# Four nested products instead of two in the last two groups of a token-mixing product, with operand sums on GpSimd

## The chip, the cores and the metric

The kernel runs on one core of one Trainium2 chip. The metric is the time of one execution in device microseconds. Each timed run gives one number, and the median of the runs stands for the kernel. The profile is one further execution, taken by the hardware profiler.

## What is computed

The reference is a linear attention block followed by a gated mixer, on 2048 tokens of width 512. Cut to the part that the change touches (`A` is the attention, `ln` a layer norm):

```
h  = x + A(ln(x))                                  # 2048 x 512
z  = gelu(ln(h) @ w_in)                            # 2048 x 1792
z1 = z[..., :Fh];  z2 = ln(z[..., Fh:])            # Fh = 896 columns each
g  = einsum('ts,sf->tf', w_sp, z2) + b_sp[:, None] # 2048 x 2048 times 2048 x 896
h2 = h + (z1 * g) @ w_out                          # 896 x 512
```

The product with `w_sp` mixes tokens. It is the largest product of the kernel, and it is the one that the change works on.

## The kernel before

All data stay in SBUF between the stages. Tokens are cut into 16 tiles of 128. The stages follow each other and overlap at their seams: attention (about the first 65 us), the product with `w_in` (to about 130 us), then the mixing product and the product with `w_out`, interleaved, to the end.

**The mixing product.** The 16 output tiles of `g` are taken as eight pairs (i, i+8), and two pairs make a group. `MIX` names the order: the groups are tiles (0, 1), (2, 3), (7, 4), (5, 6), each with its partner 8 higher. `mix` (L1042) computes one group. For each pair it uses a Strassen-Winograd scheme on 2 x 2 blocks: seven block products instead of eight. A block product of one pair is 8 matmuls of 128 x 448 columns, accumulated in a PSUM bank. The blocks of the left matrix are `wt[i]` and `wt[i+8]` (transposed `w_sp`) and their sums `sa`; those of the right matrix are `z2` and its sums `zt1`, `zt2`, `zt4`. The sums of operands are made by VectorE (DVE) with `comb` (L861), which adds or subtracts two bf16 tiles in SBUF. ScalarE (ACT) copies PSUM banks where a partial result is needed twice.

**Nesting.** A block product that both pairs of a group do against the same right block can be nested once more: `nested` (L1017) treats the two tiles as one 2 x 2 problem, and does 7 quarter products of 4 matmuls of 128 x 224 columns. It needs four sums of the left operands (`u`, tiles named nu, 512 elements per partition each), four sums of the right operand (`v`, tiles named nv, 896 elements each, made once by `quarter_sums`, L1010), four PSUM copies by ACT, and two additions in PSUM by DVE (L1026). `NEST` (L969) is a bit mask for each group: bit 1 nests the product of the first blocks, bit 2 nests the product of the sums `sa` with `zt1`. Before, it is (0, 3, 3, 3): none in the first group, two products in each later one.

**Gates.** A finished quarter of `g` gets its bias and is multiplied into `z1`. `gate` (L995) does that in one DVE instruction from PSUM (L997). `gate_p` (L1002) adds a bias-carrying copy `p` that ACT made (L1070), in one DVE instruction from PSUM (L1005), and multiplies in a second one in SBUF (L1006). A finished row of `z1` is transposed to `zgT` by a DMA on SyncE's queue (SP).

**Output product.** `mo_pair` (L1110) multiplies two `zgT` tiles with `w_out`, again by a seven-product scheme, in banks 6 and 7; its DVE evacuations are L1127 and L1139. Its operand sums (tiles us) are made by `comb` too. The last pair goes through `mo` (L1101).

**What sets the order.** Every operation is recorded first, with the operations that it depends on (data, and reuse of the same SBUF or PSUM place). `ORDER` (L16) is a packed list, written out in advance, of the sequence in which all recorded operations are emitted; each engine runs its own operations in that order. Waits come from the recorded dependencies. So a change of the operations needs a new list, and the new list may move anything. GpSimd (POOL) does small statistics of the layer norms up to about 120 us and nothing after.

The quarter sums lie in places that are dead by then: `nv1` in that of `win1`, `nv5` in that of `hnT`.

Of the kernel before, what the change touches and what calls it, by code (L numbers as in the profile page):

```python
# [252 lines left out]
def bass_sequential_preLN__linear_attn_block__mixer_gmlp__prompt_kernel(  # L253
# [14 lines left out]
    H = 32  # L268
# [733 lines left out]
    def gate_p(n, c, b, p):  # L1002
# [14 lines left out]
    def nested(X, Y, xa, xb, z, u, v, p):  # L1017
        X0, X1, Y0, Y1 = (bank(q, HQ, f) for q in (X, Y) for f in (0, HQ))
        r11, r12, r21, r22 = (x_[:, k:k + H4, :] for x_ in (xa, xb) for k in (0, H4))
        comb(u[0], r21, r22, ALU.add)  # L1020
        comb(u[1], u[0], r11, ALU.subtract)
        comb(u[2], r11, r21, ALU.subtract)
        comb(u[3], r12, u[1], ALU.subtract)
# [12 lines left out]
        copy(Y0, Y1)  # L1036
        add(Y1)
        prod(X1, u[3], z[:, H4:HT, HQ:HW], **onto)
        add(X1)
        prod(Y0, r22, v[3], **onto)  # L1040

    def mix(ia, ib, nest):  # L1042
        ss = range(HT)
        sets = ((ia, 0), (ib, 1))
        Y = {}
        for i, c in sets:
            Y[i] = tuple(wt[n][:, s:s + HT, :] for n in (i, i + HT) for s in (0, HT))
# [39 lines left out]
    DH2 = D // 2  # L1087
# [70 lines left out]
    wout_sums()  # L1158
# [36 lines left out]
```

## Time and profile before

| | |
|---|---|
| median of 3 runs | 227.19 us (227.16 to 227.52) |
| profiled execution | 227.34 us |
| its span, first to last instruction | 225.6 us |
| TensorE (PE) busy | 217.9 us, 97% |
| DVE busy | 193.5 us, 86% |
| ACT busy | 130.8 us, 58% |
| POOL busy | 51.3 us, 23% |
| granted TensorE clock | 1.00 in every stage |

A row of the timeline reads: start in us, length in us, engine, line, operation, output and inputs, shape, and how many equal instructions were merged. Matmuls are pipelined, so the length of a matmul row contains the end of the pipeline; what a group of matmuls costs is the distance from its start to the next start. The same holds for DVE rows, which overlap by some 0.08 us. A table by stage gives the busy time of each engine in stretches of the span. In the list of groups, "x16 | 10.9, 681" means sixteen instructions, 10.9 us busy in all, 681 ns each.

### The profile page before, as it was taken

Reading aid. Unit: us, or ns where it says so; the run is one execution under the profiler, and the core shown is the slowest. Engines: PE = TensorE matmul, PEld = TensorE weight load, DVE = VectorE, ACT = ScalarE, POOL = GpSimd, SP = SyncE. Lnnn points to the kernel's source line nnn. Section 1 sums busy time; section 2 is a strip of 40 time slices with the busy share of each in tenths; the row PEclk is TensorE's granted clock in tenths of the full one; section 3 lists DMA queues with packets and bytes.
Section 4 is the critical chain, followed back from the end, with each engine's and each line's share of the span. In section 5 each row is a group of like instructions: output and inputs, shape, how many; then the busy total and the mean of one; then the engine's idle time right before and its main releaser. Section 6 shows DMA issues by size and latency. Waiting matters only on the chain.

```text
span 225.6 us, 3738 instructions
## 1 busy us (share of the span) xinstructions
PE 217.9 (97%) x1311; PEld 123.0 (54%) x1325; DVE 193.5 (86%) x441; ACT 130.8 (58%) x256; POOL 51.3 (23%) x134
## 2 busy tenths in 40 slices
PE   8999999999989999999999999999999999999995
PEld 7534444453334444545555555766667667665653
DVE  3898855699989999999999999998899867497784
ACT  5686745479979999999773436624126222414111
POOL 2454400000368475786720000000000000000000
DMA  5836479937453255588930446999086109220663
GB/s 164 251 93 147 81 213 256 218 73 167 114 119 70 57 102 78 119 180 159 187 128 0 87 97 122 164 189 163 6 147 105 46 0 120 51 42 32 169 145 99
DMA packets 73906, 26.85 MB, mean 119 GB/s; under 512 B 63648, under 2 KB 73888, under 8 KB 73888
## 3 DMA queue, kind: packets, MB, share of 16 engines
q1 hardware_dynamic: 73184, 26.03, 54.9%
q10 hardware_dynamic: 704, 0.59, 0.8%
q8 instruction: 10, 0.16, 0.3%
q14 instruction: 8, 0.07, 0.1%
HBM read 6.95 MB, written 2.10 MB: 40 GB/s over the span
## 4 chain that ended last, share of the span: by engine, by line
PE 83%; DMA 6%; DVE 5%; ACT 3%; SPq 1%; issue 1%; ACTq 0%
PE psum L425 75%; PE psum L682 6%; DMA x<-in_A_x_dram 3%; DMA r<-rcp 2%; DMA zgT<-z1t 1%; DVE st L533 1%; DVE h L1139 1%; ACT ct L444 1%; ACT e L444 1%; SPq L790 1%; DVE z1t L997 1%; DVE pqT L815 1%; DVE psum L864 1%; SPq L455 1%; ACT z1t L444 0%
## 5 line engine op out<-in xcount | busy, mean ns | idle before, releaser
L444 ACT ACTIVATE psum<-psum 128x448 f32<-128x448 f32 (+2 forms) x67 | 28.5, 436 | 48.0 <-PE psum L425 40.8
L425 PE MATMUL psum<-z,wt 128*128 128x448 bf16 (+1 forms) x232 | 46.2, 343 | 0.0
L425 PEld LDWEIGHTS psum<-z,wt 128*128 128x128 bf16 x232 | 22.7, 98 | 17.3
L425 PE MATMUL psum<-win,hnT 128*128 128x448 bf16 x112 | 26.3, 353 | 0.0
L444 ACT ACTIVATE e<-psum 128x1024 bf16<-128x1024 f32 (+1 forms) x18 | 16.7, 929 | 14.1 <-PE psum L425 13.5
L444 ACT ACTIVATE z1t<-psum 128x448 bf16<-128x448 f32 (+1 forms) x24 | 16.2, 679 | 12.1 <-PE psum L425 10.1
L425 PE MATMUL psum<-zt,sa 128*128 128x448 bf16 (+1 forms) x116 | 21.7, 323 | 0.1
L425 PE MATMUL psum<-ws,hs 128*128 128x448 bf16 x72 | 18.9, 353 | 0.0
L425 PEld LDWEIGHTS psum<-win,hnT 128*128 128x128 bf16 x112 | 10.8, 98 | 10.6 <-ACT z L444 0.7
L425 PE MATMUL psum<-m,pqT 128*128 128x512 bf16 x63 | 14.7, 380 | 1.2 <-DVE pqT L815 1.0
L864 DVE TENSOR_TENSOR psum<-psum,p5z 128x448 f32<-128x448 f32 x24 | 15.0, 626 | 0.7 <-ACT z1t L444 0.5
L425 PE MATMUL psum<-wqkv,xnT 128*128 128x512 bf16 x62 | 14.9, 379 | 0.5 <-DMA wqkv<-in_A_wqkv_dram 0.5
L425 PE MATMUL psum<-xnT,wqkv 128*128 128x512 bf16 x61 | 15.0, 379 | 0.2
L682 PE MATMUL psum<-pk,xn 128*128 128x512 bf16 x63 | 15.1, 379 | 0.1
L444 ACT ACTIVATE z<-psum 128x896 bf16<-128x896 f32 x16 | 15.1, 955 | 0.1
L425 PEld LDWEIGHTS psum<-zt,sa 128*128 128x128 bf16 x116 | 11.3, 98 | 7.0
L997 DVE SCALAR_TENSOR_TENSOR z1t<-psum,b,z1t 128x448 bf16<-128x448 f32 x16 | 10.9, 681 | 3.7 <-PE psum L425 3.6
L557 POOL TENSOR_SCALAR st<-st 128x1 f32<-128x1 f32 x10 | 4.1, 410 | 42.7 <-ACT sh L444 37.1
L604 DVE TENSOR_SCALAR e<-e 128x1024 bf16<-128x1024 bf16 (+1 forms) x18 | 7.1, 395 | 7.7 <-ACT e L444 7.6
L425 PE MATMUL psum<-zt,wt 128*128 128x448 bf16 x64 | 13.4, 352 | 0.0
L533 DVE BATCH_NORM_STATS2 st<-x 128x6 f32<-128x512 bf16 x15 | 9.7, 680 | 4.1 <-DMA x<-in_A_x_dram 4.1
L425 PE MATMUL psum<-wout,zgT 128*128 128x256 bf16 (+1 forms) x71 | 13.0, 295 | 0.2 <-DVE h L1139 0.2
(145 smaller groups left out, 433.8 us busy)
## 6 DMA issues: line engine op xcount, KB each, us to landing
r<-rcp SPq DMA_DIRECT2D x16, 128.0 KB, 2.7
out_dram<-h SPq DMA_DIRECT2D x15, 128.0 KB, 1.8
win<-in_B_w_in_dram SPq DMA_DIRECT2D x2, 896.0 KB, 6.4
x<-in_A_x_dram SPq DMA_DIRECT2D x6, 256.0 KB, 4.0
wqkv<-in_A_wqkv_dram SPq DMA_DIRECT2D x2, 512.0 KB, 4.2
wout<-in_B_w_out_dram SPq DMA_DIRECT2D x1, 896.0 KB, 6.4
wo<-in_A_wo_dram SPq DMA_DIRECT2D x1, 512.0 KB, 4.9
wt<-in_B_w_sp_dram SPq DMA_TRANSPOSE x32, 3.9
```

The lines of the kernel that those rows point to most:

```text
L425: inst = pe.matmul(out_ap, lhsT=a, rhs=b, start=start and i == 0, stop=stop and i == len(pairs) - 1, **kw)
L444: return g.add("ACT", lambda ac: ac.activation(out_ap, in_ap, func, **kw), [in_ap, *extra], [out_ap] + ([accum] if accum is not None else []),
L455: return g.add(eng, lambda q: q.dma_start(out_ap, in_ap), [in_ap], [out_ap], cost=issue, lat=lat, dma=name, **k)
L533: dve(lambda v: v.bn_stats(s[:, 0:6], src[:, n, :]), [src[:, n, :]], [s[:, 0:6]], D)
L557: pool(lambda p: p.tensor_scalar(s[:, 2:3], s[:, 0:1], s[:, 0:1], -1.0 / (n * n), op0=ALU.mult, op1=ALU.mult), [s[:, 0:1]], [s[:, 2:3]], 240)
L604: dve(lambda v: v.tensor_scalar(e, e, 1.0, EPS_PHI, op0=ALU.min, op1=ALU.add), [e], [e], w * GW, acc=4)
L682: inst = pe.matmul(bank(CB[c]), lhsT=xn[:, i, c * P:(c + 1) * P], rhs=pk[:, i, :], start=i == 0, stop=i == NT - 1)
L790: g.add("SP", lambda q: q.dma_start(dst, src_ap), [rcp[:, i:i + w, :]], [dst], cost=700, lat=2200, dma=f"r{tg}{c // 2}").soft.add(win_last.i)
L815: dve(lambda v, q=q, r=r: v.tensor_tensor(q, q, r, ALU.mult), [q, r], [q], 2 * GW, acc=2)
L864: dve(lambda v: v.tensor_tensor(half(b), half(src), p, ALU.add), [half(src), p], [half(b)], HW, ps=True)
L997: dve(lambda v: v.scalar_tensor_tensor(o, half(b), b32[:, n:n + 1], o, op0=ALU.add, op1=ALU.mult), [half(b), b32[:, n:n + 1], o], [o], HW, ...
L1139: dve(lambda v, o=o, q=q, add=add: v.tensor_tensor(o, q, add, ALU.add), [q, add], [o], DH2, ps=True)
```

## The change

In the third and fourth group (tiles 7, 4 and 5, 6 with their partners) two more block products are nested: the one of the upper left tiles' second blocks with the lower half of `z2` (bit 4), and the one of the lower tiles' second blocks with `zt4` (bit 8). The operands of these products are summed by GpSimd instead of DVE: a tensor_tensor for each of the 4 + 4 quarter sums of the right operands (`nv2`, `nv4`, 896 elements per partition, once) and of the 4 left sums of each of the four nested products (512 elements), 24 instructions in all. Since a nested product ends in a bank of its own and no longer accumulates onto the others, `gate_two` brings it in: ACT copies the other part with the bias, and DVE adds and multiplies (two instructions instead of one). The four `nv2` tiles lie in the free halves of the places of `wt[2]`, `wt[3]`, `wt[10]`, `wt[11]`, and the `nv4` tiles in the places of `z1[2]`, `z1[3]`, `z1[10]`, `z1[11]`, so both wait for the second group to be done with these. The left sums use the same buffers `nu1` and `nu5` as the nested products of bits 1 and 2. The other sums of `quarter_sums` and `nested` become calls of `sums` in the same way as the first of each, which the diff shows. `ORDER` is a new list.

```diff
+    nv2 = [g.sbuf(f"nv2{k}", o_wsp + n * S * 2 + ZR, [HT // 2, HW // 2], BF16) for k, n in enumerate((2, 3, HT + 2, HT + 3))]
+    nv4 = [g.sbuf(f"nv4{k}", o_xnT + slot[n] * ZR, [HT // 2, HW // 2], BF16) for k, n in enumerate((2, 3, HT + 2, HT + 3))]
...
-    NEST = (0, 3, 3, 3)
+    NEST, ONPOOL = (0, 3, 15, 15), (4, 8, 14, 18)
...
+    def gate_two(n, c, b, e, p):
+        act(p, half(e), ACT.Identity, HW, bias=b32[:, n:n + 1], extra=[b32[:, n:n + 1]])
+        gate_p(n, c, b, p)
...
+    def sums(out_ap, a, b, op, on_pool):
+        if on_pool:
+            n = out_ap.shape[1] * out_ap.shape[2]
+            pool(lambda v: v.tensor_tensor(out_ap, a, b, op), [a, b], [out_ap], 1.75 * n)
+        else:
+            comb(out_ap, a, b, op)
...
-    def quarter_sums(v, z):
+    def quarter_sums(v, z, on_pool=False):
...
-        comb(v[0], y12, y11, ALU.subtract)
...
+        sums(v[0], y12, y11, ALU.subtract, on_pool)
...
-    def nested(X, Y, xa, xb, z, u, v, p):
+    def nested(X, Y, xa, xb, z, u, v, p, on_pool=False):
...
-        comb(u[0], r21, r22, ALU.add)
...
+        sums(u[0], r21, r22, ALU.add, on_pool)
...
+        if nest & 4:
+            nested(SETS[0] + 2, SETS[1] + 2, wt[ia][:, HT:NT, :], wt[ib][:, HT:NT, :], z2[:, HT:NT, lo], nu1, nv2, np1,
+                   4 in ONPOOL)
+            for i, c in sets:
+                gate_two(i, lo, SETS[c] + 1, SETS[c] + 2, p5[c][0])
...
-            matmuls(half(A), [(wt[tl][:, HT + s, :], z2[:, HT + s, lo]) for s in ss], **onto)
-            gate(tl, lo, A)
+            if not nest & 4:
+                matmuls(half(A), [(wt[tl][:, HT + s, :], z2[:, HT + s, lo]) for s in ss], **onto)
+                gate(tl, lo, A)
...
-            matmuls(half(B), [(wt[th][:, HT + s, :], zt4[:, s, :]) for s in ss], **onto)
-            gate(th, lo, B)
-            dma_t(zgT[th], z1[th], f"zg{th}", issue=1300, lat=1750)
+            if not nest & 8:
+                matmuls(half(B), [(wt[th][:, HT + s, :], zt4[:, s, :]) for s in ss], **onto)
+                gate(th, lo, B)
+                dma_t(zgT[th], z1[th], f"zg{th}", issue=1300, lat=1750)
+        if nest & 8:
+            ha, hb = ia + HT, ib + HT
+            nested(SETS[0] + 2, SETS[1] + 2, wt[ha][:, HT:NT, :], wt[hb][:, HT:NT, :], zt4, nu5, nv4, np5, 8 in ONPOOL)
+            for i, c in sets:
+                gate_two(i + HT, lo, SETS[c], SETS[c] + 2, p5[c][0])
+                dma_t(zgT[i + HT], z1[i + HT], f"zg{i + HT}", issue=1300, lat=1750)
...
+        if k == 2:
+            if any(m & 4 for m in NEST):
+                quarter_sums(nv2, z2[:, HT:NT, lo], 14 in ONPOOL)
+            if any(m & 8 for m in NEST):
+                quarter_sums(nv4, zt4, 18 in ONPOOL)
```

More of the change, by code (lines that the diff above doesn't have):

```diff
@@ L15 @@
 SEM_NS = 45.0
-ORDER = "c-jTQ0{{>P6a~PCziijC?Ut9ZY}+ljjAa{Z%eHN|)t0rIZQHm52qOVfAth2HkOtY24%tu<Iq(E3BP;Tt64FA*i(JTu+{lmgD1a)+i9)D~!gv}rQ47^j5JgcPMbI3zQ3A!#6d6zhEl?cI&;xZ)5~Yw4y^skl(F&ze7QK-SJy92B&<B0d8s*RqPhm9rp&k-qB>JO1+Mq4Qpgh`R6rRCYbVO!6iw+ow1!#bA$byC#fbkfFC(#KL&>0hv7|F2^jj#yMqXN2MF&d*QwxS8PV+kf<FovKThGHqYBM~NJ3Wi}BUchp^h#lC5ofwWQn2Hs+ggMxSJ(z~wn2o)78JF=Ap2KvEz+B8g61;+an1}h;kE^(b19%myuo5@00UMDNtFZ|)u?A}~3x}{72XPo%a00L4B#vMmQs5NU<0d}EXE=&;IE~M724`^{w{ad9a0|z92N!W1ckw#z;UOMj7vIEV+{Ye1z*~3&U*Jo8kKOzhKj3YAhxhOfzQVhBA75i1zrhFC&qVwYiJ6*7cz{144L`(3_!a+PFMq~CCg*SX8-F4#KgKWk7r!F~lkyY%g=G8>U>2sL`3F)mBSkU;pJY0gV`e_Z;1ev$VocAh%+9A-g9(_BnV5&gS%T%6gN>P!)mV}>nT>gwkG0r@71)fWSej*6fL+;~1zC}uSc$n<owZqqb(xzjSeZ@Pnf2I>^_iaoScqL%g#$U5<2Z!f*^m=imcMd4tFj0Svj?ByP`2cF_GBww=JTAxUL3?LY{cH2%RW5M`Fx2D*qUv)n!~t&ZMl*Y_%2`O8V=_LcHnco%1NBZg?yW<*pBaU1g~*2FL4T|@)f?rkzC8)*paXDBG>T)e#k|9jlc6c`}2MF<wv~7_Pnf*d7poB8W-~`-r%zw#p(Q-V>pWs_&3+HAD8eC-sD4m!&`ivH#L?^2}ytPAAU>fNm<KSR{t`qHgF>|Yc&7kCO)Aun#~zp!P`urEc%4mRZibAltT%XO*wUkiS#LFGNqo<W<KIw=2Af=Rw{kZLQ1V4SW#(IUWHXz6_iBPw3QuINspOUNmW&&R77vEik?<=EoXZbRZYFf&$xx@w2d9~0z2stN2-esvzBt}bB<OG9bqy3$fK;SW9+Q1`hssVy~eANx@nC1sknaPSk+N?l~5ji$%&exk~+?}*jPU^gX*fknkb{jDVg%BsU|3s)@rKq=~*4uBqi4`JfRaDpyxGNrIbP^wS&#HTJ<ztYjlzWHBI$(N;C9~^6L~&bAx7TkP7Iu)~Sa!YL?Dup*E?3)@zqatDzRDxdv;qzS9=%)(`5b#hR^NI>X*-p+5RvKkAxZ)>+Qc9?jJdZPicet6wxvOVm=W^t0w`sFvziEz@4@(`(wv-}HyJ>31#He*LNI`b!5iOs{CW{?-DW;|~3!i)yVG^p5`3L9NhL!8`S$4(YJ|6MaQT^pZZ*CB3RPlEZgo57!N~)f2v}+e+Y-x}`*ZR|)-|p3^;jp!<4XA1kqwI+>5^6SeXKCGkVOuCp4UkCfagox+dwsoLq7QaQChQ#F6CRZ8nLPUpw^Lg}5+&E3WsoXKx0i!(dBYxxbe^IQ5-Pdab3_BmyBd1rGDzpbzJm2&zU)pl-Ib}r{}2Ul@Nf2;GV>w=Njb)4T9RL>RM*`1uv1>D62UEMWY$ZcKUMWe8vaaR{{O?Pv9S9D`Hak0n~y<F9m+{_K!-7P%O#iMXEbR+k6i5TP_?(34#-{alXMLod%+|v1?P%LsW&-3%nAA?=oYyF&`b*U)fNq*XkT{@Pyr%QT-%ft}(agnGVW#g$>>iJ&gaxu;mJ;4QHgU5QPOSwjrkLBLvQLYdRJlX5~f-A*BSB_y`;ccGc?H=ulvDrI4)hqp?OM9ft_^5YyhO0*H*yvR*>zN+oN8aM$p61=&>gj$ucKHj>@*cnBno%cayPVhfxc9nUJmoiBH}?5}>qY%I=>0z7XX2_GM2A@ILq6hKao7#xnCG~C%ypAE<!f#hRiaU}j23a)>)kjyMbmi2&ErcmUiBGwj<4N1e)P9K>5g&MKlx>!_YJp+YVnrec9-ZHL!(>V^abDYyZ+AIqeuMWp7EOR`e$GFWA};M{@!o8SM-bF@r?(>v+<7Kckj64_x!8-M*sN0m;9kW@o&E9!7(gG#K^ek2ObnZ_;<IBQSpZ_`){A~=ok|p`MLPiW8-s=i-><bKK}H7o)FK+<oMW*i7_o6dTQMFUq&Q|Niikn#})tU*`b&dpLu2^jRi3;62^>J7;__S42eatIFd#3NEEMoNo<Ivks>z6vRDym;)!@E(#7gX9n0e@zYwb;eWZ*G@nUR>m60(L$GXTAYa&~0iOsP!)<*W&7TY6p?21{jBT_|{crtcI&e$D$B1!Cv6Ok(h#(|g~Ibv_@kArbI4#oO78D}DE9F1d<JI=<rI30K5Qk;(qaWO8({Wub*;%;1tR`E(4kC)>?+>2{*J+8*9@mf5L8*wXc#_MrA9>wGMAKF=C4*"
@@ new lines @@
+ORDER = "c-jTQ0{|EY5Cp)x-Tm0MZMU&)+je88v2EM7ZQFKZo1HO>Xl}H~mcSxe6w7JROqS5%S$qpDsU@?-mfK*tEQ#f@L>9vGT53yfDJ-hxvox093R!eZX{juo6|lk<!^&GlOKTaef~B`gR?r$*6U$(kEsIsQ##Y3tSX0YtF)fxgv#M6qnp-BzX4$QVwXkB=(yCc;t8O{0n{~0jESz<<64uJPTWqUowJeVHu-aC~dRiMRX{D^RwYIue#@gCg8*RNTuKjIgt(?`fkT%A~Ss$x!y=|#2vwv;8wX+G<-Wu3HHqjQ_B<pLFZHX<nhStHRT7T<j18jw@v{ly8rr0nWZlNuV9kK&9&{o?)J8UCtnjNt<*2y~CS_^MS?U)U+!M4th+ekZQGwg&-x6?M$M%gTzZ%=Ht&9fmk)E3x6TV(&)23v0%ZM$u<Z8pcA+DY4CbM2XJww<=iBG_)*W6$lZ?X`Wj-(J{DJ7ZhyoNcx9cEMKoWxHZG?5eHwi+0Vf+bR!buk4cDv|IMh!rD5&ZEx+K-M80v$L`u23+17GjlZ|m{=p*qG7sYq?4yPEDE`?Z_*!4@U+kxa^M@AJA6Zm?Y`-j~f43O^$$r>xGyiIFJet%0*f)bm@`#?@<GMVZyT|tEp2Gvr=kYwf7xWMw(ldBQPvA*Cmgo0OUe+`Fa!=^-J&PCea{iYm^W>h@EBN1D(Gz)2&*cTYu;=#jUf=6@Vo&8oJc+09)Lz$%dP;BLdAyis^Ss{LD|tI_;|;yCxA)>+!s~fyPwS05jhFPE-p3pJQt#!Ty{{kiCSJwc`fwlRRlSTK@)5q*r}<1D?f-aF@8G@tj!*Z0y_(PR!#>iR`B5L^rF@^?@)>^D`}q;?@6~;Pcl26*%v<^azwO6;wtw;a-pM=rS3lt=y@q%3IsU*0`hLIXwf&)g^Mh#a7yOZb_pW}*2l-fU<)<;uU-(7;;g|fU&-Ke57d3snzw~)N*k5@I@9snWiobTiFyDvyZ~x`lu)rN}oQRD-9v~iicpPL!0-W{`2nk_=PxQzB))OK=CizuA;|o1I5+M|xctk`(H_w4o7~+W$8GqrL|K~aJ)X(}kPmSvy8dLn8FZTQhgER<>_nr%jJRG7RFaAbtbVXX^Ljg?n^M1pZcunL+7eqxK)IuR_@DH92;qlSypdOMS8YX*P6ht=^MiD&oq$q=AsE-CHiWW$Z?udY!-Vi-d49U?Gy$~JGy+2YQ24bQt%3-5tz-(;tmMD);-W#pZ8e8!%QlbL3p%40DCNiQTGGPz~VgP2LFScVa=Ak&+pc3X{4u+sIHhX3?!cN4(d^E;Tl)x6>fh=f(G1!H%Sb(Njfs$y8H&}>qIEpHGhqqXS@!0Cyyd6qmCEDXXj$;-6!7xm~2Q0=Xltwd5#1fpqb{~$97=h1NjW1Y(k*JDq_=*cyib+_D?>LMdei5Uv4nHv&N6;Lju?#zX3f5znpTd4D$1iliZ~VYi82?}cHsTl#;3}%2Bb+BO4I;P+hp-vDy)&lc94>)8iz^6N9U&NsXK)=Mc^T&sniaXnZ{QJj<0iuL7CPZE!f*zzAsoXqBA*}vYv2xUBNFrTKSbtTL}e6i!Ba%zGu%UT#$<QhM-}ct48~#{#%5e5;B(YsJjQ22KEOj%V{X1gBL2m~Ow1a5fh4TWzgdKJ`3l8Ym3xttd6<kvnVcz@lXdtS#aWLjnTiG2Td7%sCD~7DSe^A*hy_`eHJO+DP>v0lmX+97-BgOD*@WrXkWJZNWmthN*_y4Gi*4AP6Pb@~S)MJ}i0Ro=UD!vJ*^`aAn3L3r|1bk5ae$h!J*Ti22dOKkvLkzFG6$+1J9CISupg&!Bxi82F0l`na2cmFBmdP*4%IA<P&ba!ey-sP_GKpa(qzr%O3r6y&f#2+ReyHpJg((1P0?`mW)=?S0*=v0E#d(7;Bv0xY98b?jn;aO;zn-ZW&X<{oUTnA&0(CNRUE_39Iv6Ap_$skSsKo5+|Db^%2nFQf!xXwJj@+Dz_FaIT|B~t+{2@sqw74z6FkJJI?lOTpc_2NL0qJH8qYwdc$V`OQ!lwtOSDu=xmc?eT5ENVr+JZQxI!1WPV1G8=ed_*v|P8iK{pvoo3v5aSWH*Bn<4ayw|R%z`I>jRMqw3B`}l}C7+#z8m|L_}q4bvTIF3)aP45{}I}}fc^ojrR4L@+Zc4?0$@FOGWGk0pY_Ua42Gom8tm=frS4rsrME3%^ME92+~59=GF=su(A7mw>VPv|F4DUlxV4^QeLV<@hk@u*y;#5%3#e8D7&ucSJoggUF_N~Q}sr>x4R6w0oYN~7~it5iy_)PgSRlI}6OZt1epiTX>KltZy~RabOff2)LUD5o;(nsTYM@+i0RYNaOXp6=^`3MzvNDWCGIp6=+Tis-fqsH_gEsOqb*9;$)LX`G(uDIcknGU~C)=s%UzT{TpBRZtd574=lrR9(+iLyh!NjkQcK^-M4HN=;Nr&GlJL^;*r;LT~h5U-d~f^-XQ`MV0kVE%jZs)mH8GLqAnTt@Mwo>X&}2gZ`+s+Nq8@$pQp*RZE@afdU30f*|OqF6yd~L8KsD5ITq)gbDU3Sr8=%A4Cgc1W|+NLBt?JkTQrFgbKn2v4Z5mTYXTRAYKqVNEO5l5(Wu^_(6&wO^_r=9V8AC1!;qHLDJxV%hQZr"
@@ L1006, in gate_p @@
         dve(lambda v: v.tensor_tensor(o, u, o, ALU.mult), [u, o], [o], HW, acc=2)
+    def gate_two(n, c, b, e, p):
+        act(p, half(e), ACT.Identity, HW, bias=b32[:, n:n + 1], extra=[b32[:, n:n + 1]])
+        gate_p(n, c, b, p)
     HQ, H4 = HW // 2, HT // 2
-    def quarter_sums(v, z):
-        y11, y12, y21, y22 = (z[:, k:k + H4, f:f + HQ] for k in (0, H4) for f in (0, HQ))
-        comb(v[0], y12, y11, ALU.subtract)
-        comb(v[1], y22, v[0], ALU.subtract)
-        comb(v[2], y22, y12, ALU.subtract)
-        comb(v[3], y21, v[1], ALU.subtract)
-    def nested(X, Y, xa, xb, z, u, v, p):
+    def sums(out_ap, a, b, op, on_pool):
[5 more added lines that the diff above has]
+    def quarter_sums(v, z, on_pool=False):
+        y11, y12, y21, y22 = (z[:, k:k + H4, f:f + HQ] for k in (0, H4) for f in (0, HQ))
+        sums(v[0], y12, y11, ALU.subtract, on_pool)
+        sums(v[1], y22, v[0], ALU.subtract, on_pool)
+        sums(v[2], y22, y12, ALU.subtract, on_pool)
+        sums(v[3], y21, v[1], ALU.subtract, on_pool)
+    def nested(X, Y, xa, xb, z, u, v, p, on_pool=False):
         X0, X1, Y0, Y1 = (bank(q, HQ, f) for q in (X, Y) for f in (0, HQ))
         r11, r12, r21, r22 = (x_[:, k:k + H4, :] for x_ in (xa, xb) for k in (0, H4))
-        comb(u[0], r21, r22, ALU.add)
-        comb(u[1], u[0], r11, ALU.subtract)
-        comb(u[2], r11, r21, ALU.subtract)
-        comb(u[3], r12, u[1], ALU.subtract)
+        sums(u[0], r21, r22, ALU.add, on_pool)
+        sums(u[1], u[0], r11, ALU.subtract, on_pool)
+        sums(u[2], r11, r21, ALU.subtract, on_pool)
+        sums(u[3], r12, u[1], ALU.subtract, on_pool)
         ks = range(H4)
@@ L1048, in mix @@
         if nest & 1:
-            nested(SETS[0] + 1, SETS[1] + 1, wt[ia][:, 0:HT, :], wt[ib][:, 0:HT, :], z2[:, 0:HT, lo], nu1, nv1, np1)
+            nested(SETS[0] + 1, SETS[1] + 1, wt[ia][:, 0:HT, :], wt[ib][:, 0:HT, :], z2[:, 0:HT, lo], nu1, nv1, np1,
+                   1 in ONPOOL)
         for i, c in sets:
@@ L1057, in mix @@
             comb(sa[c][1], sa[c][0], y11, ALU.subtract)
-            if not nest & 2:
-                q1 = sa[c][0]
-                matmuls(half(E), [(q1[:, s, :], zt1[:, s, :]) for s in ss])
+        if nest & 4:
[3 more added lines that the diff above has]
+                gate_two(i, lo, SETS[c] + 1, SETS[c] + 2, p5[c][0])
+        if not nest & 2:
+            for i, c in sets:
+                matmuls(half(SETS[c] + 2), [(sa[c][0][:, s, :], zt1[:, s, :]) for s in ss])
         if nest & 2:
-            nested(SETS[0] + 2, SETS[1] + 2, sa[0][0], sa[1][0], zt1, nu5, nv5, np5)
+            nested(SETS[0] + 2, SETS[1] + 2, sa[0][0], sa[1][0], zt1, nu5, nv5, np5, 2 in ONPOOL)
         for i, c in sets:
@@ L1073, in mix @@
             matmuls(half(B), [(q2[:, s, :], zt2[:, s, :]) for s in ss], **onto)
-            matmuls(half(A), [(wt[tl][:, HT + s, :], z2[:, HT + s, lo]) for s in ss], **onto)
-            gate(tl, lo, A)
+            if not nest & 4:
+                matmuls(half(A), [(wt[tl][:, HT + s, :], z2[:, HT + s, lo]) for s in ss], **onto)
+                gate(tl, lo, A)
+        for i, c in sets:
+            B, A, E = SETS[c], SETS[c] + 1, SETS[c] + 2
+            tl, th = i, i + HT
+            pa, pb = p5[c]
             copy(half(E), half(B))
@@ L1081, in mix @@
             gate_p(th, hi, B, pb)
-            matmuls(half(B), [(wt[th][:, HT + s, :], zt4[:, s, :]) for s in ss], **onto)
-            gate(th, lo, B)
-            dma_t(zgT[th], z1[th], f"zg{th}", issue=1300, lat=1750)
+            if not nest & 8:
[5 more added lines that the diff above has]
+            nested(SETS[0] + 2, SETS[1] + 2, wt[ha][:, HT:NT, :], wt[hb][:, HT:NT, :], zt4, nu5, nv4, np5, 8 in ONPOOL)
+            for i, c in sets:
+                gate_two(i + HT, lo, SETS[c], SETS[c] + 2, p5[c][0])
+                dma_t(zgT[i + HT], z1[i + HT], f"zg{i + HT}", issue=1300, lat=1750)
     DH2 = D // 2
```

## The prediction

> **What bounds the kernel now.** I read the chain of work that ended last, then the busy times by stage, then the timelines of PE, DVE and POOL.
>
> ```profile
> PE 83%; DMA 6%; DVE 5%; ACT 3%; SPq 1%; issue 1%; ACTq 0%
> ```
>
> PE is 83% of the chain. After 67 us the chain stays on PE but for short pieces of DVE, ACT and a DMA near 133 to 140 us and near 215 us. The change works in the last third, so here are its stages (busy us of PE, PEld, DVE, ACT and POOL):
>
> ```profile
> 132.00:152.00 20.00, 19.57 (x137) 12.69 (x137) 19.74 (x44) 9.98 (x23) 0.00 (x0) 1.00 0.78 145
> 152.00:168.00 16.00, 15.95 (x109) 10.57 (x109) 14.28 (x37) 4.93 (x14) 0.00 (x0) 1.00 0.63 103
> 168.00:185.00 17.00, 16.95 (x118) 11.35 (x118) 13.81 (x34) 6.73 (x16) 0.00 (x0) 1.00 0.35 61
> 185.00:208.00 23.00, 22.84 (x160) 15.65 (x162) 17.41 (x45) 7.92 (x19) 0.00 (x0) 1.00 0.36 59
> ```
>
> PE never rests from 152 to 208 us, at full clock. DVE is the second engine: full to 152 us, then 89%, 81% and 76%. ACT has over half of its time free, POOL all. So a matmul saved here is time saved, as long as DVE, which rests 1.7, 3.2 and 5.6 us in the last three of these stages, and now POOL keep up.
>
> **What is removed.** One block product, before and after, from the PE rows:
>
> ```profile
> 186.21 0.55 PE L425 MATMUL psum<-z,wt 128*128 128x224 bf16 x4
> 186.59 0.55 PE L425 MATMUL psum<-zt,sa 128*128 128x224 bf16 x4
> 186.97 0.49 PE L425 MATMUL psum<-vs,zgT 128*128 128x256 bf16 x3
> 187.30 0.38 PE L425 MATMUL psum<-wout,zgT 128*128 128x512 bf16 x1
> 187.52 1.68 PE L425 MATMUL psum<-zt,wt 128*128 128x448 bf16 x8
> 189.03 0.55 PE L425 MATMUL psum<-nv,nu 128*128 128x224 bf16 x4
> ```
>
> Start to start, 4 matmuls of 224 columns cost 0.38 to 0.39 us and 8 of 448 cost 1.51 us. Two plain products of a group are 2 x 1.51 = 3.02 us; nested they are 7 x 0.385 = 2.70 us. That saves 0.32 us, four times: **1.3 us** of PE. I find no other change of PE's work.
>
> **What is added, off POOL.** Each nested product has 4 ACT copies (0.34 us) and 2 Identity copies (0.58 us): 2.5 us, 10 us in all, beside ACT's 36 us of rest from 152 to 208 us; I cost it at nothing. On DVE each adds 2 PSUM additions (L1026, a pair takes 0.70 us) and turns two L997 (0.68 us) into L1005 and L1006 (0.62 and 0.39 us, overlapping by 0.1): 0.65 + 2 x 0.25 = 1.15 us, 4.6 us in all. DVE's 10.5 us of rest would cover that alone.
>
> **What POOL gets.** 24 sums, 8 of 896 and 16 of 512 elements, behind all its old work, which ends at about 120 us; nothing old waits for them. No row shows such a POOL instruction. The nearest for size write only: 0.204 us for 128 elements (L462) and 0.104 us for 8 (L470), so 0.83 ns per element; a two-input instruction on 2 elements takes 0.20 us (L566). From below that is one pass, 0.93 and 0.61 us; from above three (two reads and a write), 2.42 and 1.46 us. I take two passes, for the two inputs: **1.68 and 1.04 us**. [...]
>
> New waits: a left sum waits for the nested product that used its buffer (nu1, nu5) before, whichever engine made it, and the other way round: DVE's next sums into nu1, nu5 and sa10 wait for POOL, with gates and evacuations queued behind them, and PE for those. On SP the last half of wt[6] and wt[14] now stand behind the zgT transposes of tiles 3 and 11, whose gates end near 168 us by the places below. At 1.3 us to issue each (2.66 us for two at 166.79) and 3.9 us to land, they are there by 176 us; the first sums of them that PE needs are due at 185 to 190. I cost that at nothing; each us that the gates slip takes one of these ten.
>
> **POOL against DVE.** Two pairs of timelines:
>
> ```profile
> 81.37 2.24 POOL L569 TENSOR_TENSOR rs<-st,expo 128x2 f32<-128x2 f32 x1
> ```
> ```profile
> 81.36 0.68 DVE L861 TENSOR_TENSOR wt<-wt,wt 128x1024 bf16<-128x1024 bf16 x1
> 81.95 0.42 DVE L861 TENSOR_TENSOR hs<-hs,hnT 128x512 bf16<-128x512 bf16 x1
> 82.28 0.42 DVE L861 TENSOR_TENSOR hs<-hnT 128x512 bf16<-128x512 bf16 x1
> 82.62 0.42 DVE L861 TENSOR_TENSOR hs<-hnT,hs 128x512 bf16<-128x512 bf16 x1
> ```
>
> L569 takes 0.71 us where DVE reads PSUM or does statistics. Here it started 10 ns behind the first of four DVE sums with both inputs in SBUF, and ended 0.57 us behind the last: it waited through all four. Likewise L559 takes 0.30 us, and 1.25 us (at 103.51) beside the 1.09 us sum at 103.58, ending 0.09 us behind it. So such a DVE sum and a POOL instruction that reads SBUF exclude each other. That a long POOL instruction holds DVE in turn is not shown: POOL's old operands are 1 or 2 elements. I take the exclusion both ways. [...]
>
> Now places, by adding these PE durations along the changed order from its last shared point (131.76 us, the first group's last product):
>
> - First nested product of bit 4. POOL's nv21 overwrites `wt[3]`, read until 160.1 us. PE needs nv22 and nu12 at 165.8. POOL does nv21, nv22, nu12 in that order: 2 x 1.68 + 1.04 = 4.4 us. DVE has sa11, nu52 and wt7 in a row there (0.59 + 0.33 + 0.59 = 1.5 us) and a short one (0.3) behind; POOL waits for these. 160.2 + 4.4 + 1.8 = 166.4, with semaphores 166.6: PE waits **0.8 us**.
> - 168 to 185 us (16.7 us of PE). DVE's rows of the new order are 42 instructions: 6.9 us with PSUM, 9.0 us of SBUF sums; 15.9 in all. POOL has four sums of 896 and six of 512: 12.9 us. The 9.0 and 12.9 us exclude each other: 21.9 us in 16.7, 5.2 too much. POOL's last ones are due 1 to 5 us later and its first may start earlier, so I take half: **2.6 us**, which DVE falls behind and PE waits for, through the us, nu and evacuations queued behind each held sum.
> - After 185 us eight sums of 512 remain (8.3 us) over 23 us, where DVE has room: nothing.
> - The end. The last gate grows from 0.68 to 0.64 + 0.62 + 0.39 us, and PE has 4.2 us of other work between the last product and its transposed result, 0.5 less than before. That chain (0.7 + 0.2, 2.9 us for the DMA) had 0.9 us to spare of 4.7: now 0.5 short, of which the earlier waits hide little. I take **0.4 us**.
> - The head of the new order differs little on PE up to 75 us; the bias's transpose now stands ahead of the r loads, where SP rested from 45 to 50 us. Nothing, within 0.3 us either way.
>
> Sum: 227.34 - 1.3 + 0.8 + 2.6 + 0.4 = 229.8 us. The profiled execution lies 0.15 us over the median of the runs, so I say **229.7 us**. With a quarter or all of the 5.2 us, 228.4 to 232.3.
>
> **Rivals.**
> 1. *Faster, 225.9 us.* A POOL sum costs DVE nothing, because it keeps the read only briefly, and is short enough. For it: at 63.84 us POOL's L573 (0.57 us) began 12 ns ahead of a DVE sum, which took 0.72 us against 0.68. Against: its one operand is read at once. It decides below some 1.2 us for 896 elements: then 2 x 1.2 + 0.8 + 1.8 us fit between 160.2 and 165.8. The 1.3 us are kept, and the end's 0.4 us too is taken as hidden.
> 2. *Nearly nothing, 227.1 us.* DVE is never held, but POOL waits for runs of DVE sums and is late for the first product: -1.3 + 0.8 + 0.4.
> 3. *Much slower, 234.2 us.* Three passes per element. The middle stretch has 9.0 + 18.4 - 16.7 = 10.7 us too much, half is 5.3; the first product waits 2.6 us: -1.3 + 5.3 + 2.6 + 0.4 = +7.0.
>
> That the change does not do what it says can be left out: the changed order shows the 24 sums on POOL and the 4 x 28 matmuls of 224 columns.
>
> **How the numbers follow.** Forecast 0.50, rival 1 0.22, rival 2 0.13, rival 3 0.15. The range goes from 225.7 (rival 1, with most of the head's 0.3 gained) to 233.5, which leaves out most of rival 3. About 0.2% is what a measurement of this kernel can tell from no change. Faster by more: rival 1 and a little of 2, 0.24; within: 0.09 of rival 2; slower: 0.67.
>
> **What would show it.** Right: POOL sums near 1.7 and 1.0 us alone and far longer beside DVE sums; DVE sums in SBUF of 0.69 us that take 1 to 2 us from 152 to 185 us; PE waiting for nu12 near 166 us and for DVE's sums after. Wrong: DVE's sums as long as before, PE without a gap to 208 us, or POOL sums of 1 us.

## The result and the profile after

The changed kernel takes **243.34 us** (median of 4 runs, 242.97 to 243.68), the kernel before 227.34 us on the same chip (227.16 to 227.52). The ratio is 1.071, with an interval of 1.069 to 1.073. I had said 229.7 us, within 225.7 to 233.5. The direction was right; the loss is 16.0 us where I had 2.5. The profiled execution has a span of 241.1 us (before: 225.6).

The chain of work that ended last, by engine, was 83% PE before. After:

```profile
PE 61%; DVE 25%; DMA 6%; ACT 4%; issue 2%; SPq 1%; DVEq 0%; ACTq 0%
```

A quarter of the chain is now DVE. The stages in which PE never rested before (busy us of PE, PEld, DVE, ACT and POOL, then PE's clock, the DMA share and GB/s):

```profile
152.00:168.00 16.00, 11.79 (x84) 7.60 (x82) 16.00 (x23) 3.57 (x10) 11.44 (x7) 1.00 0.28 30
168.00:185.00 17.00, 10.90 (x88) 7.96 (x86) 15.46 (x21) 4.72 (x13) 11.85 (x7) 1.00 0.54 96
185.00:208.00 23.00, 20.47 (x143) 14.19 (x144) 20.79 (x46) 9.48 (x24) 8.14 (x6) 0.93 0.01 3
```

PE rests 4.2, 6.1 and 2.5 us. DVE is busy throughout the first stage, and yet completes 23 instructions where it completed 37 before: its instructions got longer, not more. The timeline of DVE, and that of POOL for the same time, show why:

```profile
162.51 1.73 DVE L863 TENSOR_TENSOR us<-zgT,zgT 128x384 bf16<-128x384 bf16 x1
164.16 2.06 DVE L1008 TENSOR_TENSOR z1t<-u,z1t 128x448 bf16<-128x448 bf16 x1
```
```profile
162.02 2.01 POOL L1019 TENSOR_TENSOR nv<-z,nv 128x896 bf16<-128x896 bf16 x1 [0.58 <-PE psum L427]
163.99 1.98 POOL L1019 TENSOR_TENSOR nv<-z 128x896 bf16<-128x896 bf16 x1
```

The same two kinds in the kernel before:

```profile
166.68 0.39 DVE L1006 TENSOR_TENSOR z1t<-u,z1t 128x448 bf16<-128x448 bf16 x1
...
170.08 0.35 DVE L861 TENSOR_TENSOR us<-zgT,zgT 128x384 bf16<-128x384 bf16 x1
```

The us sum took 0.35 us before, the multiplication into z1 0.386. In the changed kernel each now starts inside a POOL sum and ends about 0.2 us behind that sum's end; POOL's next sum starts at once and holds DVE's next one. I call "held time" what the DVE instructions with two SBUF inputs took beyond the mean of their shape before. After 130 us it is 17.9 us in 17 instructions: 6.7 us in the first stage above, 6.9 in the second, 3.4 in the third, 1.0 later. Before, it was nothing. POOL's 24 sums took 36.9 us, added up one by one. DVE instructions that read PSUM kept their length (L1007 0.616 us, L1005 before 0.621).

PE waits for DVE and not for POOL: from 150 us on its waits are 12.8 us for DVE and 0.9 us for ACT, and no wait of PE or of DVE ends with a POOL sum. Its gaps of 1.5 us and more, in square brackets with what ended them:

```profile
158.55 0.50 PE L427 MATMUL psum<-wout,us 128*128 128x256 bf16 x3 [1.59 <-DVE us L863]
...
166.91 0.72 PE L427 MATMUL psum<-wout,zgT 128*128 128x256 bf16 x4 [2.42 <-DVE h L1170]
...
175.73 0.56 PE L427 MATMUL psum<-nv,wt 128*128 128x224 bf16 x4 [1.87 <-DVE psum L1039]
...
179.97 0.49 PE L427 MATMUL psum<-wout,us 128*128 128x256 bf16 x3 [1.50 <-DVE us L863]
...
185.91 0.81 PE L427 MATMUL psum<-wout,zgT 128*128 128x256 bf16 x3 [3.21 <-DVE h L1170]
```

L1170 and L1039 read PSUM and were not held themselves (0.42 and 0.39 us, as before: 0.42 and 0.395); they stood in DVE's queue behind sums that were. Ahead of the last gap DVE also waited 1.30 us for a wt load.

### The profile page after: what moved, and what is told of

It is laid out like the page before. It is cut to its first block, busy times and chain, and to the rows that moved or that the text cites. A ratio compares the mean times of both kernels' runs of the same rounds, so it can differ in the third digit from the quotient of the medians.

```text
span 241.1 us, 3947 instructions
## 1 busy us (share of the span) xinstructions
PE 221.7 (92%) x1373; PEld 126.1 (52%) x1373; DVE 216.9 (90%) x457; ACT 140.4 (58%) x280; POOL 88.8 (37%) x158
## 4 chain that ended last, share of the span: by engine, by line
PE 61%; DVE 25%; DMA 6%; ACT 4%; issue 2%; SPq 1%; DVEq 0%; ACTq 0%
PE psum L427 54%; PE psum L684 6%; DVE us L863 4%; DVE sa L863 3%; DMA x<-in_A_x_dram 2%; DVE z1t L1008 2%; DVE wt L863 2%; DMA wt<-in_B_w_sp_dram 2%; DVE h L1170 2%; DVE u L1007 2%; DVE nu L863 1%; DVE psum L1039 1%; DMA zgT<-z1t 1%; DVE z1t L999 1%; DVE st L535 1%
## 5 line engine op out<-in xcount | busy, mean ns | idle before, releaser
L446 ACT ACTIVATE psum<-psum 128x224 f32<-128x224 f32 (+2 forms) x79 | 32.3, 420 | 48.7 <-PE psum L427 36.2
L427 PE MATMUL psum<-z,wt 128*128 128x448 bf16 (+1 forms) x216 | 41.7, 335 | 0.0
L427 PEld LDWEIGHTS psum<-z,wt 128*128 128x128 bf16 x216 | 21.0, 98 | 15.4 <-DVE u L1007 0.2
L427 PE MATMUL psum<-win,hnT 128*128 128x448 bf16 x112 | 25.6, 353 | 0.0
L446 ACT ACTIVATE e<-psum 128x1024 bf16<-128x1024 f32 (+1 forms) x18 | 16.7, 930 | 13.6 <-PE psum L427 12.9
L446 ACT ACTIVATE p<-psum,b 128x448 f32<-128x448 f32 x24 | 14.6, 634 | 14.7 <-DVE psum L1039 7.8
L427 PE MATMUL psum<-zt,sa 128*128 128x448 bf16 (+1 forms) x124 | 22.8, 323 | 0.1
L427 PE MATMUL psum<-wout,zgT 128*128 128x256 bf16 (+1 forms) x77 | 15.6, 307 | 6.2 <-DVE h L1170 6.2
L1007 DVE TENSOR_TENSOR u<-psum,p 128x448 bf16<-128x448 f32 x24 | 14.7, 617 | 4.2 <-PE psum L427 3.5
L1019 POOL TENSOR_TENSOR nv<-z 128x896 bf16<-128x896 bf16 x2 | 4.1, 2061 | 38.5 <-PE psum L427 38.5
L427 PE MATMUL psum<-nv,nu 128*128 128x224 bf16 x120 | 16.7, 264 | 0.9 <-ACT psum L446 0.9
L427 PE MATMUL psum<-m,pqT 128*128 128x512 bf16 x64 | 14.8, 380 | 0.4 <-DVE pqT L817 0.3
L446 ACT ACTIVATE z<-psum 128x896 bf16<-128x896 f32 x16 | 14.6, 932 | 0.0
```

The source lines that it names most:

```text
L427: inst = pe.matmul(out_ap, lhsT=a, rhs=b, start=start and i == 0, stop=stop and i == len(pairs) - 1, **kw)
L446: return g.add("ACT", lambda ac: ac.activation(out_ap, in_ap, func, **kw), [in_ap, *extra], [out_ap] + ([accum] if accum is not None else []),
L1019: pool(lambda v: v.tensor_tensor(out_ap, a, b, op), [a, b], [out_ap], 1.75 * n)
```

## The experiments

Three theories went in. **Theory 1:** POOL's long sums hold DVE's SBUF sums, and DVE becomes the bound. **Theory 2:** POOL's results come late. **Theory 3:** the new order itself costs, with the last wt loads behind zgT transposes on SP. The chain after speaks for 1 and 3: it runs through a wt load issued at 176.65 us, behind transposes that waited for gates.

### 1. All sums on DVE

```diff
-    NEST, ONPOOL = (0, 3, 15, 15), (4, 8, 14, 18)
+    NEST, ONPOOL = (0, 3, 15, 15), ()
```

> The 24 sums are made by DVE instead of POOL, in the same order of all operations. Theory 1 (POOL's long sums hold DVE's SBUF sums, and DVE becomes the bound): the 17.9 us that DVE was held go, and DVE gets 8 x 0.54 + 16 x 0.34 = 9.8 us of sums of its own; with the 4.6 us of gates and additions that is 14.4 us against 10.5 us of rest, so some 4 us too much and 228 to 233 us. Theory 2 (POOL's results come late, and the engines wait for them): DVE's sums are three times shorter, so 226 to 228 us. Theory 3 (the new order itself, with its later gates and the loads of wt behind zgT transposes on SP): 238 us or more.

Measured: 237.3 us, ratio 1.047 (1.041 to 1.054), no DVE sum held. So some 6 us of the loss went with POOL's sums, but fewer than theory 1 had said: the time lies between the forecasts of theories 1 and 3. Part of the rest is the loads (experiment 7).

### 2. The order alone

```diff
-            pool(lambda v: v.tensor_tensor(out_ap, a, b, op), [a, b], [out_ap], 1.75 * n)
+            pool(lambda v: v.memset(out_ap[:, 0:1, 0:8], 0.01), [a, b], [out_ap], 1.75 * n)
...
+        if on_pool:
+            u = (r21, r11, r22, r12)
+            v = [z[:, k:k + H4, f:f + HQ] for k in (0, H4) for f in (0, HQ)]
```

> Each POOL sum becomes a write of 8 elements (some 0.1 us), and the nested products read raw blocks of wt and z instead of POOL's results, so nobody waits for POOL; the order, the nesting, the gates and the SP queue stay as in the changed kernel. The sums are left out, so the output differs. Theory 1 and theory 2: 225.5 to 227.5 us, the four nested products' 1.3 us less than before, plus at most 1 us at the end. Theory 3: 236 us or more.

Measured: 230.2 us, ratio 1.014 (1.010 to 1.018). That is between the forecasts: theory 3 is not the main cause, but the order costs something by itself. PE lost 2.6 us in one place, and the chain says where:

```profile
168.72 0.43 DVE nu L870
169.15 0.91 SPq L467
...
170.10 4.79 DMA wt<-in_B_w_sp_dram
...
175.26 0.68 DVE sa L870
175.94 0.67 DVE h L1182 x2
```

The DVE row behind this load:

```profile
174.91 0.43 DVE L870 TENSOR_TENSOR nu<-wt 128x512 bf16<-128x512 bf16 x1 [3.30 <-DMA wt<-in_B_w_sp_dram]
```

DVE reaches this nu sum at 171.6 us and waits for the second half of wt[6], which SP issues only at 170.1 us, behind the zgT transposes. The evacuation of h that PE waits for is queued behind it. By its operands the sum needs only the first half, issued at 162.19 us. But the kernel counts both loads of a tile in one semaphore and waits for the full count (L219 and L232 of the kernel before).

### 3. Everyone waits for POOL, but it only writes

```diff
-            pool(lambda v: v.tensor_tensor(out_ap, a, b, op), [a, b], [out_ap], 1.75 * n)
+            parts = [(k, f) for k in range(4) for f in range(0, w, 64)]
...
+                for k, f in parts:
+                    r = v.memset(out_ap[:, k:k + 1, f:min(f + 64, w)], 0.01)
```

> Each POOL sum becomes a run of writes of 64 elements that fills the same tile (about 16 x 0.15 us for 896 elements, 8 x 0.15 us for 512): POOL is as late as with the sums, everyone waits for it as in the changed kernel, but it reads nothing in SBUF. The sums are left out, so the output differs. Theory 1: no DVE sum is held, 226 to 229 us. Theory 2: 238 to 244 us, as the changed kernel. Theory 3: 238 us or more.

Measured: 230.55 us, ratio 1.017 (1.014 to 1.020): 0.4 us more than the order alone, which the intervals do not tell from nothing, and 1.6 us above theory 1's range, which had left out the cost of the order. POOL was busy for 22.2 us in this phase, against 36.6 us in the changed kernel: a write lasts 0.15 us but starts 0.08 us after the one before, so a tile of 896 elements is full after 1.34 us where the sum took 2.0. Every operation depended on POOL as in the changed kernel, though POOL was less late than there. So this run speaks against theory 2 only in part; experiment 4 is the full test. No DVE sum was held. POOL and DVE, side by side:

```profile
160.43 2.62 POOL L1024 MEMSET nv<- 128x64 bf16 x32 [1.14 <-PE psum L427]
```
```profile
161.30 0.68 DVE L863 TENSOR_TENSOR sa<-sa,wt 128x1024 bf16<-128x1024 bf16 x1
161.90 0.42 DVE L863 TENSOR_TENSOR nu<-sa,sa 128x512 bf16<-128x512 bf16 x1
162.23 0.69 DVE L863 TENSOR_TENSOR wt<-wt,sa 128x1024 bf16<-128x1024 bf16 x1
```

The three sums keep the 0.69 and 0.42 us that they took before. So POOL's writes held no DVE sum here, in 22.2 us of POOL; its reads did, for 20.2 us in experiment 4 and 6.5 us in experiment 9.

### 4. The sums, but nobody waits for them

```diff
+        if on_pool:
+            u = [t[:, :, 0:P] for t in v]
...
+            u = (r21, r11, r22, r12)
+            v = [z[:, k:k + H4, f:f + HQ] for k in (0, H4) for f in (0, HQ)]
```

POOL's left sums go into the nv tiles, which no product reads here, and so POOL does the quarter sums of a kind ahead of the left sums (in experiments 2, 6, 8 and 9 too). The order of DVE's operations stays.

> POOL does its 24 sums of 896 and 512 elements, but the nested products read raw blocks instead of them, and POOL's left sums go into places that only POOL uses; so no engine waits for POOL, by data or by a buffer. The nested products have other operands, so the output differs. Theory 1: DVE's SBUF sums are held for 10 to 18 us in all, 234 to 242 us. Theory 2: 225.5 to 229 us. Theory 3: 238 us or more, with DVE's sums not held.

Measured: **244.35 us**, ratio 1.078 (1.075 to 1.081), held time 20.2 us. No engine waits for POOL, and the whole loss is there. The stages:

```profile
168.00:185.00 17.00, 11.30 (x77) 8.00 (x77) 16.76 (x19) 4.38 (x11) 15.34 (x11) 0.90 0.42 74
185.00:208.00 23.00, 18.06 (x124) 12.33 (x125) 22.20 (x42) 8.00 (x20) 13.47 (x10) 0.93 0.00 1
```

DVE is as good as full and PE rests 5.7 and 4.9 us. Experiment 2 is the same kernel without the sums, and takes 14.2 us less; this settles theory 1 against theory 2. The time came out 2 us above the upper end that I had given for theory 1.

### 5 to 7. The last wt loads issued early

The same move in three kernels: the four loads (here by number) stand in SP's order ahead of the zgT transposes of tiles 2 and 10.

```diff
+        for i in (819, 820, 821, 822):
+            ids.remove(i)
+            ids.insert(ids.index(889), i)
```

In the changed kernel:

> The changed kernel with one move: the last four loads of wt (the two halves of wt[6] and of wt[14]) stand on SP ahead of the zgT transposes of tiles 2 and 10, so they no longer wait for gates. The run of the order alone lost 2.6 us of PE near 176 us to these loads. Theory 1 (held DVE sums cost nearly all, the loads are a loss of their own on top): 2 to 4 us less than the changed kernel, 239 to 242 us, with DVE's sums held as before. Rival (most of the loss runs through the loads, since held DVE sums make the gates slip and with them the loads): 229 to 235 us.

Measured: 243.95 us, ratio 1.071 (1.068 to 1.074): no gain. In this kernel the loads only waited in parallel with a DVE that was late anyway (held time 19.3 us). Both forecasts missed.

In the order alone:

> The order alone (POOL does next to nothing, nobody waits for it, sums left out, so the output differs), with the same four loads moved ahead. If the loads were the whole loss of the order alone: 2.5 us less than its 230.2 us, 227 to 228 us, and PE without a gap from 168 to 185 us. If DVE's added gates and additions cost something beside it (the 4.6 us that the prediction costed at nothing): 229 to 230.5 us, with the gap still there behind another DVE instruction.

Measured: 226.63 us, ratio **0.997** (0.995 to 0.999), a little under the first forecast. The 2.6 us are gone:

```profile
152.00:168.00 16.00, 16.00 (x119) 11.35 (x117) 14.56 (x35) 4.76 (x15) 0.95 (x11) 1.00 0.60 97
168.00:185.00 17.00, 17.00 (x143) 13.54 (x141) 14.80 (x38) 9.33 (x24) 0.94 (x13) 1.00 0.14 28
185.00:208.00 23.00, 23.00 (x185) 17.55 (x183) 19.96 (x53) 12.53 (x30) 0.00 (x0) 1.00 0.50 92
```

PE has no gap in 56 us, and the kernel is 0.8 us faster than before. That is what four more nested products are worth if their operands cost nothing; they are left out here, so it is no kernel to use. From here to the changed kernel with early loads are 243.95 - 226.63 = 17.3 us, for making the sums on POOL.

With all sums on DVE:

> All 24 sums on DVE, and the same four loads moved ahead. If DVE's own 9.8 us cost about 5 us as DVE is then the bound, and the loads 2 to 3 us: 233 to 235.5 us. If the loads were most of what the sums on DVE cost (the late gates again): 228 to 231 us.

Measured: 233.7 us, ratio 1.027 (1.025 to 1.030), some 4 us less than with the loads late (3.6 by the times, 4.6 by the ratios), as the first forecast had it. Against 226.63 us, 9.8 us of sums on DVE cost 7.1 us:

```profile
168.00:185.00 17.00, 14.86 (x118) 10.96 (x117) 16.92 (x43) 8.30 (x21) 0.00 (x0) 1.00 0.15 28
185.00:208.00 23.00, 20.17 (x166) 15.36 (x163) 20.55 (x57) 11.34 (x29) 0.00 (x0) 1.00 0.31 62
```

DVE is full in the first of these stages, and in the second PE loses 2.8 us though DVE rests 2.4. So DVE's rest was not a store that any added work could draw on here.

### 8 and 9. How much POOL reads

Half the columns of each sum, and a copy of one operand instead of a sum; both on the kernel of experiment 4, in which nobody waits.

```diff
-            pool(lambda v: v.tensor_tensor(out_ap, a, b, op), [a, b], [out_ap], 1.75 * n)
+            pool(lambda v: v.tensor_tensor(out_ap[:, :, 0:w], a[:, :, 0:w], b[:, :, 0:w], op), [a, b], [out_ap], 1.75 * n)   # 8
+            pool(lambda v: v.tensor_copy(out_ap, a), [a, b], [out_ap], 1.75 * n)   # 9
```

> Nobody waits for POOL, as in the run of that name (244.4 us), and each POOL sum is done on half of its columns (448 and 256 elements instead of 896 and 512), so POOL reads half as long. The sums are not used, so the output differs. Theory 1 with a price in proportion to POOL's reading time: halfway between the order alone (230.2) and 244.4, 236 to 239 us, and 8 to 12 us of held DVE time. If DVE's rest hides the first half: 230 to 233 us. If the number of POOL instructions counts and not their length: 241 us or more.

Measured: 231.6 us, ratio 1.018 (1.014 to 1.022).

> Nobody waits for POOL, and each POOL sum becomes a copy of one of its operands into the same place (one input of 896 or 512 elements instead of two). The copies are not used, so the output differs. The long writes held no DVE sum in 37.8 us of POOL, the sums held 20.2 us in 37.5. If any reading of SBUF by POOL holds DVE's sums: at 0.9 and 0.5 us each, some 15 us of POOL and 4 to 8 us of held DVE time, which is what half the sums did, so 230.5 to 233 us. If only two inputs hold: nothing held, 229.5 to 230.5 us, as the order alone (230.2 us).

Measured: 231.0 us, ratio 1.019 (1.015 to 1.024). A copy held DVE as well, 6.5 us in all. (The 37.8 us in this expectation add up writes that overlap; POOL was busy with them for 22.2 us.) POOL and DVE in turn; z1t took 0.39 us before and nu 0.42:

```profile
168.02 0.62 POOL L1026 COPY nv<-wt 128x512 bf16<-128x512 bf16 x1
168.59 2.15 POOL L1026 COPY nv<-zt 128x896 bf16<-128x896 bf16 x2
```
```profile
168.09 0.79 DVE L1015 TENSOR_TENSOR z1t<-u,z1t 128x448 bf16<-128x448 bf16 x1
168.81 0.38 DVE L1051 TENSOR_TENSOR psum<-psum,np 128x224 f32<-128x224 f32 x1
169.11 0.84 DVE L870 TENSOR_TENSOR nu<-nu,sa 128x512 bf16<-128x512 bf16 x1
```

Put together, with POOL's busy time from 130 us on (overlaps counted once):

| POOL does | POOL busy | DVE held | over the order alone (230.2 us) |
|---|---|---|---|
| long writes (experiment 3) | 22.2 us | 0 | 0.4 us |
| copies (9) | 20.5 us | 6.5 us | 0.8 us |
| half sums (8) | 22.5 us | 7.1 us | 1.4 us |
| whole sums (4) | 37.1 us | 20.2 us | 14.2 us |

The first three rows differ by less than the intervals, about 1 us either way, can tell. The price is not in proportion: 6 to 7 us of held time were nearly free, and the 13 us beyond cost 13 us. "If DVE's rest hides the first half" was the forecast that held.

### 10 and 11. Two nested products instead of four

Only bit 4, with the sums on DVE (10) or on POOL (11). Both have one and the same new order, in which the last two wt loads still stand behind zgT transposes (issued at 176.79 us in experiment 10).

```diff
-    NEST, ONPOOL = (0, 3, 15, 15), (4, 8, 14, 18)
+    NEST, ONPOOL = (0, 3, 7, 7), ()           # 10
+    NEST, ONPOOL = (0, 3, 7, 7), (4, 14)      # 11
```

> Only bit 4 nested in the last two groups (two added nested products instead of four), all its sums on DVE, in an order close to that of the kernel before. PE is saved 2 x 0.32 = 0.64 us. DVE gets 8 x 0.34 + 4 x 0.54 + 2 x 1.15 = 7.2 us more. All 14.4 us on DVE had cost 7.1 us, of which some 7 were hidden. If DVE's rest hides up to 7 us in any order: 226.5 to 227.0 us, a little less than before. If it hides less, since a DVE instruction that is late by its own work also makes PE wait: 227.5 to 229 us.

Measured: 230.1 us, ratio 1.014 (1.012 to 1.016), slower than either forecast. Not all of it is DVE's load: 1.3 us of PE's rest lies in a stretch near the first group, where the new order makes PE wait for ACT and DVE (this row of the kernel before, then of experiment 10):

```profile
132.00:140.00 8.00, 7.80 (x53) 4.70 (x51) 7.78 (x16) 4.35 (x10) 0.00 (x0) 1.00 0.47 91
```
```profile
132.00:140.00 8.00, 6.46 (x42) 3.76 (x41) 6.68 (x14) 3.36 (x8) 0.00 (x0) 1.00 0.81 125
```

So it does not show that two nested products can't pay; it shows that they did not in this order.

> The same with the 12 sums of bit 4 on POOL (4 of 896 and 8 of 512 elements, some 17.5 us of POOL at 2.0 and 1.2 us). DVE loses 4.9 us of sums of its own and is held for about half of POOL's time, 8 us, so it is 3 us worse off than in the run with these sums on DVE. Theory 1: 1 to 4 us slower than that run, 229 to 232 us. Theory 2 (a POOL sum frees DVE, the change only did too many): as fast or faster, 226 to 227.5 us.

Measured: ratio 1.037 (1.028 to 1.045), about 235.6 us by the kernel before's 227.27; the runs spread from 233.9 to 239.4, and the profiled one, at a lower mean clock (0.986), is the longest. Held time 9.7 us, by 12 POOL sums of 19.4 us in all. Between two kernels that differ in nothing but the engine of 12 sums, POOL loses by some 5 us, more than the 1 to 4 us of theory 1; theory 2's "a POOL sum frees DVE" falls. Not all of it is held time: in this profile PE also waited 1.3 us for a POOL sum (nv), and 0.7 us were lost before POOL's first sum. No version that makes all its sums beats the kernel before.

## Why the prediction was wrong

Its steps in order:

- **PE's saving of 1.3 us, and the end's loss of 0.4 us: right together.** Experiment 6 has both without the sums, and gained 0.8 us of the 0.9; its last gap of PE is 0.59 us where before had 0.24, which bears out the 0.4.
- **Added ACT and DVE work beside the sums at nothing: right**, by the same run (PE without a gap from 152 to 208 us).
- **A POOL sum of 1.68 and 1.04 us: a little low.** They take 1.88 to 2.14 us and, with little in their way, 1.15 us. The two passes were my estimate; the runs show the lengths alone. (POOL's old work ended at 114 us, not at about 120, which changes nothing here.)
- **POOL and DVE exclude each other both ways: right.** The second way was an assumption, as the trace before didn't show it. That a POOL sum under way holds a DVE sum is in the lines above: 1.73 us where the us sum took 0.35 before.
- **PE waits 0.8 us for nu12 near 166 us: wrong.** PE waits there, 2.4 us, but for DVE's L1170 behind two held instructions. No wait of PE in the changed kernel ends with a POOL sum. (The 0.2 us for semaphores in this place was my estimate, with no row beside it.)
- **168 to 185 us, 2.6 us: this is the step that failed.** I set the 9.0 us of DVE's SBUF sums and POOL's 12.9 us against 16.7 us, as if they alone shared the time, and halved the excess of 5.2. I left out the PSUM work, 6.9 us, that stands in DVE's queue behind the sums: it came late with them (PE waited 1.87 us for L1039 at 175.73, which is 0.39 us long and started as a held sum of 2.06 us ended). The sum to make is DVE's whole work plus held time against the stage. With DVE's work as experiment 6 has it and the held time that was measured: 14.8 + 6.9 = 21.7 us in 17, 4.7 too much; PE rested 6.1. Even my 5.2, not halved, would have been near this. I halved it because POOL's sums may lie earlier or later, and then costed held time in the neighbouring stages at nothing.
- **152 to 168 us and after 185 us, held time at nothing: wrong by the same omission.** I counted only POOL's lateness in the first and called the second free. In the first, 14.6 us (experiment 6) + 6.7 held = 21.3 in 16, 5.3 too much, and PE rested 4.2. In the second, 19.96 + 3.4 = 23.4 in 23, 0.4 too much, and PE rested 2.5: work that does not fit slips into the next stage, so the sum holds for the three together (10.4 us too much, 12.8 rested) better than for each.
- **The wt loads behind the transposes at nothing: wrong in itself, though not in the changed kernel.** I took their due time from PE (185 to 190 us). But DVE's queue comes to the first sum of wt[6] at 171.6 us (experiment 2), that sum waits 3.30 us for both halves, and the evacuation of h that PE waits for is queued behind it. That is some 3.5 us in the order alone (230.17 - 226.63), none where DVE is late anyway.

The held share is the number that would have sized it: held time was 49 to 54% of POOL's time in the runs with whole sums (17.9 of 36.9, 19.3 of 37.4, 20.2 of 37.5, and 9.7 of 19.4 us in experiment 11; sums added up one by one). My own 30.1 us of POOL and a half give 15 us held, of which the 5.9 us of rest that DVE kept after its 4.6 us of added work could hide some: 9 us or more of loss, not 2.6. Of my rivals the much slower one had the size nearest (234.2 us), but by POOL sums of 2.42 and 1.46 us, which took 1.88 to 2.14 and, with little in their way, 1.15. The 16.0 us are then: 17.3 us for POOL's sums, less 0.8 us that the rest gained; that is 0.5 us more than measured, which lies within the spread between chips (the kernel before ran at 226.9 to 227.4). Within the 17.3 us, the halved clock told below is one part (1.7 us by experiment 5's profile); I did not separate it further from the gaps that it follows.

## What to carry to other kernels

If DVE has sums with both inputs in SBUF at that time, moving element-wise work from DVE to POOL need not take anything off DVE. Here about half of POOL's time came back as held time, twice what DVE was spared (19.3 us for 9.8 in experiments 5 and 7, 9.7 for 4.9 in experiments 10 and 11). Set DVE's whole work plus that against the stage, since the PSUM work queued behind a held sum came late with it here (PE waited 2.42 and 3.21 us for L1170). DVE's rest hid some 6 us of held time (experiments 8 and 9) and little beyond. And take as the due time of a load the time at which the first instruction that waits for it reaches the head of its queue (171.6 us in experiment 2), not the time at which the bound engine needs the result (185 to 190).

## What I had not expected of the hardware

**After some gaps PE ran at half its clock.** In the changed kernel, behind the gap of 3.21 us that ended at 185.91:

```profile
186.00:188.00 2.00, 2.00 (x11) 1.33 (x11) 1.97 (x7) 1.15 (x2) 0.00 (x0) 0.50 0.00 0
188.00:190.00 2.00, 2.00 (x11) 1.15 (x10) 2.00 (x5) 1.97 (x6) 0.00 (x0) 0.66 0.00 0
```

The clock is 0.50 for 3.4 us, and four matmuls of 224 columns cost 0.73 us there, start to start (187.17 to 187.90), against 0.38 at full clock (159.11 to 159.49). I estimate the loss at half of the 3.4 us, 1.7 us. The same came with gaps of 3.85 and 2.29 us (experiment 4), 2.84 us (experiment 1), 2.42 us (experiment 5) and, for 6.8 us, 1.91 us (experiment 11). It did not come with one of 2.42 us at 166.91 in the changed kernel, 2.49 us at 168.26 in experiment 4 or 2.12 us in experiment 2. So the length of a single gap did not decide it in these runs; what did, none of them shows.

**What POOL read counted, and its number of inputs little.** In nearly the same busy time of POOL, copies held DVE for 6.5 us (of 20.5), half sums for 7.1 (of 22.5) and writes for nothing (of 22.2).
